# VectorE's operations for the second chunk's heads, issued behind those on the features of the first two slots

## The chip, the cores and the metric

The kernel runs on one core of a Trainium2 chip. What counts is the time of one execution on the device, in microseconds (us). Three runs of the kernel before took 885.66, 886.93 and 889.05 us; the median is 886.93.

A core has five engines, each with its own in-order queue: TensorE (PE in the profile: matrix products, with PEld for its weight loads), VectorE (DVE), ScalarE (ACT), GpSimd (POOL) and SyncE (SP), which here issues the loads and stores. An instruction starts when it has reached the head of its engine's queue and the semaphores that it waits for have been raised; all behind it on that engine wait with it.

## The reference

Two steps follow each other. The first is attention over 8 batches, 8 heads, 576 positions of 64 features; heads 0 to 3 look at the last 32 positions (local), heads 4 to 7 at the positions with the same remainder by 32 (strided). The second is a feed-forward layer on the 4608 tokens.

```python
scores = scale * np.matmul(q, k.transpose(0, 1, 3, 2))
mask_local = (rel >= 0) & (rel < stride)
mask_strided = (rel >= 0) & (pos[None, :] % stride == pos[:, None] % stride)
scores = np.where(masks[None, :, :, :], scores, -1000000000.0)
scores = scores - np.max(scores, axis=-1, keepdims=True)
attn = np.exp(scores)
attn = attn / (np.sum(attn, axis=-1, keepdims=True) + 1e-09)
x = np.matmul(attn, v)            # then laid out as 4608 tokens x 512
h = np.maximum(x @ w_in, 0.0)     # 512 -> 2048
out = h * h @ w_out               # 2048 -> 512
```

The weights w_in and w_out arrive as 64-bit floats.

## The kernel before

**Tiling.** The 4608 tokens are cut into 12 chunks of 384, each made of two segments of 192 positions of one batch. For each chunk the heads give four tiles: xlh, xll (local heads, high and low part) and xsh, xsl (strided heads). A number in 32 bits is split into a high part that TensorE's fast 32-bit format holds and a low part, the rest; a product is done as three: high with high, high weight with low x, low weight with high x. So `up` issues 12 products for one slot of 128 features (four 128-row pieces of x times three), and `down` issues 9 for one slot (three token tiles times three).

**Slots.** A chunk has 16 slots j of 128 features. `up(c, j)` makes h_j (on TensorE, L458), its squared Relu, the high part gh (ScalarE, L471) and the low part gl (VectorE, L472). `down` adds slot j's part to y (L485), two slots later in chunk 0. In chunk 0 the squared Relu is split: ScalarE makes the Relu (L466), VectorE multiplies it with h (L467), then ScalarE casts gh from that. In later chunks ScalarE does both (L469, L470).

**Weights.** They are converted on the chip during chunk 0, from 64-bit halves to high and low parts, by `convert`: ScalarE scales (L154) and prepares the low word (L166), VectorE joins the two (L169), ScalarE casts the high part (L172), GpSimd subtracts for the low part (L173). Six steps of it run ahead of the slots, then WRATE = 2 steps per slot, each issued on ScalarE behind the slot's gh. Weight pieces come in the order w_0 (of w_in), w_1, w_0 (of w_out) and so on; a piece is converted in two halves of 512 columns.

**Heads of chunk 0** are made ahead of everything, by `pe_pair` on TensorE. `heads_end` holds the last instructions of that part by engine: a for ScalarE, g for GpSimd, s for SyncE, v for VectorE.

**Heads of chunk 1.** Its local heads again go through `pe_pair` (`local`). Its strided heads go through `strided`, which uses VectorE and GpSimd and runs once per segment: for each of the six positions i of a segment in its lane GpSimd multiplies q with the keys up to i (L408), VectorE sums over the features (L409); then maximum, difference, exponential, sum and normalisation (L414 to L421); then GpSimd multiplies values with weights (L430) and VectorE sums (L431). The result is transposed (L437), cast into xsh (L441) and xsl (L442). The products of L408 and of L430 share two buffers (`prod`, bufs=2): the third product can only be written when the first has been summed. A segment's data come by one load (L388).

**What sets the order.** The program is traced in Python order, and a scheduler then orders each engine's queue; it works with estimates of times, and moves instructions between the traced places where data allow. `issue_after(ins)` binds: what is traced within it stands behind `ins` on that engine's queue. `behind(ins, gen)` applies it, for every engine in a dictionary, to each step of a generator. Up to slot LATER = 3 chunk 1's heads are not yet traced; from there on a share of them is traced in each slot, but bound only behind `heads_end`, so the scheduler may put them earlier, into the places of slots 0 to 2.

**In the names of the order** h_0 to h_15 are chunk 0's features, gh_0 and gl_0 their two parts, raw_... a weight piece on its way and w_... the converted one, z_... the prepared low word, sc_2, pq_2, pp_2 the scores, key products and value products of the first segment of chunk 1, sc_3, pq_3, pp_3 those of the second, and sc_4, pq_4 those of chunk 2. The last number of a name only tells tiles apart.

Of the kernel before, what the change touches and what calls it, by code (L numbers as in the profile page):

```python
# [49 lines left out]
def f32(ap):  # L50
    return ap.bitcast(F32)
# [23 lines left out]
def ranges(c):  # L75

    res = []
    for s, (b, g) in enumerate(SEGS[c]):
        if res and res[-1][0] == b and res[-1][2] == SI * g:
            res[-1][2] += SI  # L80
        else:
            res.append([b, SI * g, SI * (g + 1), SEG * s])
    return res
# [3 lines left out]
def attn_moe(ctx: ExitStack, tc, qk_l, v_l, qk_d, v_d, qk_p, v_p, f_s, q_s, k_s, v_s, w_in, w_out, masks, eye, out):  # L87
    nc = tc.nc
# [13 lines left out]
    def psum(i, nm):  # L102

        return ps.tile([P, 512], F32, name=nm, tag=f"ps{i}")
# [17 lines left out]
    last = {}  # L122
# [325 lines left out]
    def up(c, j):  # L448
        x = xt[c]
        p, o = divmod(j, 2)  # L450
        ph = psum((c * NFT + j) % 3, f"h{c}_{j}")
        n = 0
        for kt in range(4):
            kind, kk = "ls"[kt // 2], kt % 2
            xh, xl = x[kind, "h"][:, kk, :], x[kind, "l"][:, kk, :]
            wsl = slice(kt * 256 + o * P, kt * 256 + (o + 1) * P)
            for w, xx in ((wi[p][0], xh), (wi[p][0], xl), (wi[p][1], xh)):
                done = nc.tensor.matmul(ph[:, :TC], w[:, wsl], xx, start=n == 0, stop=n == 11)  # L458
                n += 1
        gh = gpool.tile([P, TC], F32R, name=f"gh{c}_{j}", tag="gh")  # L460
        gl = gpool.tile([P, TC], F32R, name=f"gl{c}_{j}", tag="gl")
        g = ph[:, :TC]
        if c == 0:

            r = p_t[j % 2].rearrange("p w q -> p (w q)")
            nc.scalar.activation(r, g, AF.Relu)  # L466
            nc.vector.scalar_tensor_tensor(out=g, in0=g, scalar=0.0, in1=r, op0=ALU.max, op1=ALU.mult)  # L467
        else:
            nc.scalar.activation(g, g, AF.Relu)  # L469
            nc.scalar.activation(g, g, AF.Square)  # L470
        last["gh"] = nc.scalar.copy(gh, g)  # L471
        nc.vector.tensor_sub(gl, g, f32(gh))  # L472
        g_tiles[c, j] = gh, gl
        return done

    def down(c, j):
        gh, gl = g_tiles.pop((c, j))
        p, o = divmod(j, 2)
        if j == 0:
            y_ps[c] = [ps_y.tile([P, DM], F32, name=f"y{c}_{t}", tag="psy") for t in range(NTT)]  # L480
        wsl = slice(o * DM, (o + 1) * DM)
        for t in range(NTT):
            sl = slice(t * P, (t + 1) * P)
            for k, (g, w) in enumerate(((gh, wo[p][0]), (gh, wo[p][1]), (gl, wo[p][0]))):
                done = nc.tensor.matmul(y_ps[c][t], g[:, sl], w[:, wsl], start=j == 0 and k == 0, stop=j == NFT - 1 and k == 2)  # L485
        if j == NFT - 1:
            for t in range(NTT):
                y = ypool.tile([P, DM], F32, name=f"ysb{c}_{t}", tag="ysb")
                (nc.scalar.copy if t == 1 else nc.vector.tensor_copy)(y, y_ps[c][t])
                nc.sync.dma_start(out=out[c * TC + t * P : c * TC + (t + 1) * P, :], in_=y)  # L490
        return done


    def run(gen):
        for _ in gen:
            pass

    def behind(ins, gen):

        while True:  # L500
            with ExitStack() as st:
                for i in ins.values():
                    st.enter_context(tc.issue_after(i.ins))
                try:
                    k = next(gen)
                except StopIteration:
                    return
            yield k
# [25 lines left out]
    def local(c):  # L534
        heads = [pair_at(c, pr, True, pr, "3") for pr in range(2)]
        for h in (0, 0, 1, 0, 1, 0, 0, 1, 1, 1):
            next(heads[h])
            yield
# [15 lines left out]
    def take(c, which):  # L554

        if NPLAIN <= c < NCHUNK:
            for h in map(int, which):
                if (c, h) not in heads:
                    heads[c, h] = pe_head(c, h)
                with ExitStack() as st:  # L560
                    for i in (last["pe"], *(weights_end.values() if c == NPLAIN else ())):
                        st.enter_context(tc.issue_after(i.ins))
                    last.pop("mm", None)
                    next(heads[c, h])
                    last["pe"] = last.get("mm", last["pe"])
# [51 lines left out]
    heads_end = {e: last[e] for e in "agsv"}  # L617
# [3 lines left out]
    for s in range(NS + 2):  # L621
        c, j = divmod(s, NFT)
        if s < NFT:
            up(c, j)
            if s >= 2:
                last["pe"] = down(*divmod(s - 2, NFT))

        elif s % 2 == 0:
            before, between, rest = plan[j // 2]
            for part, slots, two in (up, (s, s + 1), before), (down, (s - 2, s - 1), between):  # L630
                take(c + 1, two)
                with tc.issue_after(last["pe"].ins):
                    for i in slots:
                        if 0 <= i < NS:
                            last["mm"] = part(*divmod(i, NFT))
                last["pe"] = last["mm"]
            take(c + 1, rest)
        if j == NFT - 2:
            take(c + 2, "010")
        if c == 0:  # L640

            weights = behind({"a": last["gh"]}, ungated)
            for _ in range(WRATE):
                if next(weights, "end") != "end":
                    weights_end = {e: last[e] for e in "agsv"}
        if s == LATER:
            zbank = (4,)
        if s == NFT - 1:
            for t in p_t:
                nc.gpsimd.memset(t, 0.0)  # L650
        if c + 1 < NCHUNK and s >= LATER:
            j0 = LATER if c == 0 else 0
            if j == j0:
                lo, st = local(c + 1) if c == 0 else iter(()), strided(c + 1)
                if c == 0:
                    lo, st = behind(heads_end, lo), behind(heads_end, st)
                if c == 1:
                    st = behind(weights_end, st)
                cost = sum(2 * sum(range(i0 + 1, i1 + 1)) + 10 for _, i0, i1, _ in ranges(c + 1))
                dl = ds = 0  # L660
            fl, fs = ((j + 1 - j0) / n for n in SPREAD[min(c, 1)])
            while dl < fl * 10 and next(lo, "end") != "end":
                dl += 1
            while ds < fs * cost:
                k = next(st, "end")
                if k == "end":
                    break
                ds += k
            if j == NFT - 1:
                run(lo)  # L670
                run(st)
# [76 lines left out]
```

## Time and profile before

| | |
|---|---|
| median of three runs | 886.93 us |
| the profiled execution | 886.95 us |
| its span, first to last instruction | 885.2 us |
| mean granted TensorE clock | 0.993 |
| PE busy | 871.1 us (98%) |
| VectorE, ScalarE, GpSimd busy | 640.3, 572.1, 677.3 us |

The profile is that of one execution. The share of busy time is an average over all stages; the first 47 us (loads, heads of chunk 0, first slots) differ from the rest. In the row of the granted clock 1.00 is full speed (2.4 GHz) and 0.50 half of it. Times of instructions count from the start of the span. A row of the timeline may merge neighbours of one kind (x6); its second number then is the time from the first start to the last end.

### The profile page before, as it was taken

To read this page: it belongs to the slowest core of one execution; us is meant where nothing else is said; L and a number is where in the kernel's file an instruction comes from. 1 tells how busy PE (TensorE), PEld (TensorE's weight loads), DVE (VectorE), ACT (ScalarE), POOL (GpSimd) and SP (SyncE) were. 2 spreads that over 40 slices of the span, in tenths; PEclk is the share of its full clock that TensorE was granted. 3 is DMA by queue.
4 is the path that set the end of the run, shared out by engine and by line. 5 is a ranking of instruction groups with operands and counts; after the bars stand their busy time and mean duration, and the time that the engine had idled before them with its cause. 6 is when DMAs were issued, how large, how long until landed. Compare 5 with 4: busy or idle time off the path is not lost.

```text
span 885.2 us, 14792 instructions
## 1 busy us (share of the span) xinstructions
PE 871.1 (98%) x4744; PEld 792.5 (90%) x4744; DVE 640.3 (72%) x1820; ACT 572.1 (65%) x1510; POOL 677.3 (77%) x722
## 2 busy tenths in 40 slices
PE   8799999999999999999999999999999999999997
PEld 7688899999999999989899999999999999998996
DVE  5579677877877878878779778778787887883111
ACT  5799876666666666757757747656666665664332
POOL 4689887878987989889888988997998899782000
PEclk9899999999999999999999999999999999999999
DMA  9943441323023123104102302312021121000000
GB/s 347 361 149 107 154 150 40 103 83 113 26 71 103 45 80 107 43 13 147 47 13 79 99 29 74 90 44 74 29 98 61 31 70 61 7 2 8 29 1 36
DMA packets 26797, 71.40 MB, mean 81 GB/s; under 512 B 2976, under 2 KB 8736, under 8 KB 25184
## 3 DMA queue, kind: packets, MB, share of 16 engines
q1 hardware_dynamic: 26432, 70.14, 24.0%
q8 instruction: 37, 0.61, 0.3%
q10 hardware_dynamic: 288, 0.33, 0.1%
q14 instruction: 40, 0.33, 0.1%
HBM read 61.01 MB, written 9.44 MB: 80 GB/s over the span
## 4 chain that ended last, share of the span: by engine, by line
PE 96%; DMA 2%; ACT 1%; POOL 1%; DVE 0%; issue 0%; DVEq 0%; POOLq 0%; ACTq 0%
PE h L458 45%; PE y L485 45%; PE s L234 2%; PE o L280 2%; DMA qk<-qk_d 2%; ACT e L341 1%; PE w_ps L580 1%; PE b L317 1%; PE b L363 0%; POOL pq L408 0%; POOL w L173 0%; PE b L355 0%; DVE e L322 0%; ACT raw L154 0%; DVEq L739 0%
## 5 line engine op out<-in xcount | busy, mean ns | idle before, releaser
L485 PE MATMUL y<-w,gh 128*128 128x512 f32 x1152 | 357.5, 392 | 2.0 <-ACT gh L471 2.0
L485 PEld LDWEIGHTS y<-w,gh 128*128 128x128 f32 x1152 | 212.5, 188 | 42.2 <-ACT gh L471 2.3
L458 PE MATMUL h<-xlh,w 128*128 128x384 f32 x768 | 230.8, 341 | 1.8 <-DVE raw L169 1.8
L458 PE MATMUL h<-xsh,w 128*128 128x384 f32 x768 | 226.1, 335 | 0.0
L485 PE MATMUL y<-w,gl 128*128 128x512 f32 x576 | 224.7, 393 | 0.0
L430 POOL TENSOR_TENSOR pp<-vs,sc 128x448 f32<-128x448 f32 (+10 forms) x192 | 189.9, 1014 | 38.1 <-DVE qs L431 19.2
L408 POOL TENSOR_TENSOR pq<-ks,qs 128x512 f32<-128x512 f32 (+2 forms) x192 | 197.9, 1050 | 17.6 <-DVE sc L409 13.8
L472 DVE TENSOR_TENSOR gl<-h,gh 128x384 fp32r<-128x384 f32 x192 | 105.5, 550 | 81.3 <-ACT gh L471 80.1
L409 DVE TENSOR_REDUCE sc<-pq 128x8 f32<-128x512 f32 (+4 forms) x228 | 119.8, 535 | 50.0 <-POOL pq L408 46.9
L471 ACT CAST gh<-h 128x384 fp32r<-128x384 f32 x192 | 91.6, 478 | 98.5 <-PE y L485 96.0
L469 ACT ACTIVATE h<-h 128x384 f32<-128x384 f32 x176 | 82.9, 471 | 109.7 <-PE h L458 109.2
L458 PEld LDWEIGHTS h<-xlh,w 128*128 128x128 f32 x768 | 143.2, 190 | 4.9 <-DVE raw L169 2.0
L458 PEld LDWEIGHTS h<-xsh,w 128*128 128x128 f32 x768 | 141.9, 188 | 0.2
L431 DVE TENSOR_REDUCE qs<-pp 128x64 f32<-128x448 f32 (+11 forms) x192 | 106.7, 563 | 32.4 <-POOL pp L430 30.6
L458 PE MATMUL h<-xll,w 128*128 128x384 f32 x384 | 130.0, 339 | 0.0
L485 PEld LDWEIGHTS y<-w,gl 128*128 128x128 f32 x576 | 108.5, 188 | 23.0
L458 PE MATMUL h<-xsl,w 128*128 128x384 f32 x384 | 128.4, 335 | 0.0
L470 ACT ACTIVATE h<-h 128x384 f32<-128x384 f32 x176 | 83.3, 473 | 3.6
L259 DVE STREAM_TRANSPOSE p_t<-e 32x128 f32<-32x128 f32 x240 | 72.2, 301 | 10.5 <-ACT e L248 6.2
L458 PEld LDWEIGHTS h<-xll,w 128*128 128x128 f32 x384 | 73.1, 190 | 2.2
L458 PEld LDWEIGHTS h<-xsl,w 128*128 128x128 f32 x384 | 72.2, 188 | 0.1
L243 ACT ACTIVATE e<-e,nm 96x128 f32<-96x128 f32 x160 | 62.6, 393 | 12.9 <-DVE nm L226 11.1
(87 smaller groups left out, 1080.4 us busy)
## 6 DMA issues: line engine op xcount, KB each, us to landing
qk<-qk_l SPq DMA_DIRECT2D x24, 400.0 KB, 3.2
y<-ysb SPq DMA_DIRECT2D x36, 256.0 KB, 3.4
raw<-w_in SPq DMA_DIRECT2D x7, 1024.0 KB, 11.4
qk<-qk_l SPq DMA_DIRECT2D x16, 416.0 KB, 3.2
vs<-v_s SPq DMA_DIRECT2D x10, 576.0 KB, 4.1
raw<-w_out SPq DMA_DIRECT2D x5, 1024.0 KB, 13.3
v<-v_l SPq DMA_DIRECT2D x40, 128.0 KB, 2.1
ks<-k_s SPq DMA_DIRECT2D x8, 576.0 KB, 3.8
```

Source lines behind the costliest of these rows:

```text
L243: nc.scalar.activation(e[:QC, cut(w)], e[:QC, cut(w)], AF.Exp, bias=nmax[:QC, w : w + 1], scale=-1.0, accum_out=ssum[:QC, w, :1])
L259: nc.vector.transpose(out=pt[STR * k : STR * (k + 1), :, STR * r : STR * (r + 1)], in_=e.rearrange("p (w k) -> p w k", k=KW)[STR * r : STR ...
L408: nc.gpsimd.tensor_mul(pv, kt[:, a : a + m, :], qt[:, i - i0 : i - i0 + 1, :].broadcast_to([P, m, D]))
L409: nc.vector.tensor_reduce(out=sc[:, i - i0, a : a + m], in_=pv, op=ALU.add, axis=AX.X)
L430: nc.gpsimd.tensor_mul(pv, vt[:, a : a + nd, :n], sc[:, il : il + 1, :n].broadcast_to([P, nd, n]))
L431: nc.vector.tensor_reduce(out=ot[:, il, a : a + nd], in_=pv, op=ALU.add, axis=AX.X)
L458: done = nc.tensor.matmul(ph[:, :TC], w[:, wsl], xx, start=n == 0, stop=n == 11)
L469: nc.scalar.activation(g, g, AF.Relu)
L470: nc.scalar.activation(g, g, AF.Square)
L471: last["gh"] = nc.scalar.copy(gh, g)
L472: nc.vector.tensor_sub(gl, g, f32(gh))
L485: done = nc.tensor.matmul(y_ps[c][t], g[:, sl], w[:, wsl], start=j == 0 and k == 0, stop=j == NFT - 1 and k == 2)
```

## The change

At the end of slot 1 a second dictionary is made from `heads_end`: for VectorE it holds the instruction that makes gl of slot 1 instead of the last one of chunk 0's heads. Chunk 1's heads, local and strided, are bound behind it. For the other three engines nothing differs in the dictionary.

```diff
@@ up
         last["gh"] = nc.scalar.copy(gh, g)
-        nc.vector.tensor_sub(gl, g, f32(gh))
+        last["gl"] = nc.vector.tensor_sub(gl, g, f32(gh))
@@ the loop over slots
+        if s == 1:
+
+            slot_end = heads_end | {"v": last["gl"]}
         if s == LATER:
             zbank = (4,)
@@
                 if c == 0:
-                    lo, st = behind(heads_end, lo), behind(heads_end, st)
+                    lo, st = behind(slot_end, lo), behind(slot_end, st)
```

The scheduler orders all queues anew from this. VectorE's queue at the first slots of chunk 0, of before (-) and now (+):

```order
 L169 SCALAR_TENSOR_TENSOR raw_196<-raw_196,z_512_512 128x512
-L409 TENSOR_REDUCE sc_2_680<-pq_2_0_0_682 128x1
-L409 TENSOR_REDUCE sc_2_680<-pq_2_1_0_685 128x2
-L409 TENSOR_REDUCE sc_2_680<-pq_2_2_0_688 128x3
-L409 TENSOR_REDUCE sc_2_680<-pq_2_3_0_691 128x4
-L409 TENSOR_REDUCE sc_2_680<-pq_2_4_0_694 128x5
 L467 SCALAR_TENSOR_TENSOR h_0_517<-h_0_517,p_t_90 128x384
-L409 TENSOR_REDUCE sc_2_680<-pq_2_5_0_755 128x6
 L467 SCALAR_TENSOR_TENSOR h_1_548<-h_1_548,p_t_91 128x384
-L414 TENSOR_REDUCE mx_2_758<-sc_2_680 128x6
 L472 TENSOR_TENSOR gl_0_531<-h_0_517,gh_0_530 128x384
 L169 SCALAR_TENSOR_TENSOR raw_261<-raw_261,z_0_537 128x512
```

The first segment's six score reductions and its maximum leave this place; they now stand behind gl_1, spread among the weights' L169 and the features of slots 2 and 3.

GpSimd's queue at the same place:

```order
 L408 TENSOR_TENSOR pq_2_0_0_682<-qkvs_2_678 128x64
 L408 TENSOR_TENSOR pq_2_1_0_685<-qkvs_2_678 128x128
+L173 TENSOR_TENSOR w_0_505<-raw_196,w_0_505 128x512
+L173 TENSOR_TENSOR w_2_536<-raw_261,w_2_536 128x512
 L408 TENSOR_TENSOR pq_2_2_0_688<-qkvs_2_678 128x192
 L408 TENSOR_TENSOR pq_2_3_0_691<-qkvs_2_678 128x256
+L173 TENSOR_TENSOR w_2_536<-raw_261,w_2_536 128x512
 L408 TENSOR_TENSOR pq_2_4_0_694<-qkvs_2_678 128x320
 L408 TENSOR_TENSOR pq_2_5_0_755<-qkvs_2_678 128x384
-L173 TENSOR_TENSOR w_0_505<-raw_196,w_0_505 128x512
-L173 TENSOR_TENSOR w_2_536<-raw_261,w_2_536 128x512 x2
+L173 TENSOR_TENSOR w_1_567<-raw_263,w_1_567 128x512 x2
```

Three weight conversions have moved in among the key products. Behind this piece the conversions of w_1, w_3 and half of w_2 now follow each other, and the value products pp_2 stand behind them.

GpSimd's queue at the end of chunk 0, where the second segment's xsl is made:

```order
+L653 MEMSET p_t_90 128x384
+L653 MEMSET p_t_91 128x384
 L173 TENSOR_TENSOR w_7_1249<-raw_0_1075,w_7_1249 128x512
 L400 MEMSET sc_4_1472 128x108
 L218 TENSOR_TENSOR kx_0_1340<-qk_0_1329,kx_0_1340 128x448
+L220 TENSOR_TENSOR qx_0_1339<-qk_0_1329,qx_0_1339 64x384
 L408 TENSOR_TENSOR pq_4_0_0_1474<-qkvs_4_1470 128x64
 L408 TENSOR_TENSOR pq_4_1_0_1477<-qkvs_4_1470 128x128
-L220 TENSOR_TENSOR qx_0_1339<-qk_0_1329,qx_0_1339 64x384
 L255 TENSOR_TENSOR vx_0_1580<-v_0_1330,vx_0_1580 128x4x64
+L173 TENSOR_TENSOR w_7_1249<-raw_512_1077,w_7_1249 128x512
 L442 TENSOR_TENSOR xsl_886<-qkvs_3_951,xsh_885 128x2x192
```

The two memsets and the last weight conversion, which stood behind this L442, now stand in front of it. Elsewhere the order differs too: on PE's queue three y products of slot 2 now stand inside h_4, in front of its last four products, and on SyncE's the second segment's load (L388) stands behind the load of raw_803 instead of in front of it. The new file has three lines more, so L650 of before is L653 there.

## Rows read from the trace of the kernel before

**Rows 1.** Page: busy us (share of the span) and number of instructions by engine.

```profile
PE 871.1 (98%) x4744; PEld 792.5 (90%) x4744; DVE 640.3 (72%) x1820; ACT 572.1 (65%) x1510; POOL 677.3 (77%) x722
```

**Rows 2.** All waits of PE from 28 us on: total, times, longest, us.

```profile
PE y L485 <- ACT gh L471: 2.0, 1, 2.0
PE h L458 <- DVE raw L169: 1.8, 1, 1.8
```

**Rows 3.** Timeline of PE: start, duration, instruction, idle before it and its releaser.

```profile
18.44 1.25 PE L363 MATMUL b<-pt,v 128*64 128x96 f32 x16 [0.70 <-ACT pt L356]
...
42.51 1.94 PE L485 MATMUL y<-w,gh 128*128 128x512 f32 x6 [1.98 <-ACT gh L471]
...
48.37 1.55 PE L485 MATMUL y<-w,gh 128*128 128x512 f32 x6
...
50.45 0.33 PE L458 MATMUL h<-xlh,w 128*128 128x384 f32 x1
```

**Rows 4.** Stretches: PE, PEld, DVE, ACT, POOL busy; granted clock, DMA share, GB/s.

```profile
0.00:20.00 20.00, 16.79 (x212) 15.34 (x213) 10.30 (x23) 11.18 (x41) 6.91 (x17) 1.00 0.93 338
...
40.50:42.50 2.00, 0.03 (x1) 0.00 (x0) 1.59 (x5) 0.53 (x2) 1.40 (x2) 1.00 0.59 223
42.50:45.50 3.00, 2.99 (x9) 2.36 (x10) 2.83 (x6) 3.00 (x6) 1.33 (x1) 0.70 0.04 15
45.50:47.10 1.60, 1.60 (x6) 1.58 (x5) 1.35 (x4) 1.60 (x5) 0.53 (x1) 0.50 0.00 0
```

**Rows 5.** Timeline of VectorE in front of the first slot's feature.

```profile
40.98 0.49 DVE L409 TENSOR_REDUCE sc<-pq 128x5 f32<-128x320 f32 x1 [0.41 <-POOL pq L408]
41.38 0.56 DVE L467 SCALAR_TENSOR_TENSOR h<-h,p_t 128x384 f32<-128x384 f32 x1
```

**Rows 6.** Timeline of ScalarE: Relu, cast of gh_0, four of the weight casts.

```profile
39.52 0.87 ACT L466 ACTIVATE p_t<-h 128x384 f32<-128x384 f32 x2 [3.00 <-PE h L458]
41.98 0.48 ACT L471 CAST gh<-h 128x384 fp32r<-128x384 f32 x1 [1.58 <-DVE h L467]
...
42.91 0.65 ACT L172 CAST w<-raw 128x512 fp32r<-128x512 f32 x1
...
45.81 0.68 ACT L172 CAST w<-raw 128x512 fp32r<-128x512 f32 x1
...
49.98 0.65 ACT L172 CAST w<-raw 128x512 fp32r<-128x512 f32 x1
...
56.52 0.71 ACT L172 CAST w<-raw 128x512 fp32r<-128x512 f32 x1
```

**Rows 7.** Timeline of GpSimd: the first key products, and around the second L442.

```profile
38.12 3.78 POOL L408 TENSOR_TENSOR pq<-qkvs 128x64 f32<-128x64 f32 x6
43.64 1.33 POOL L173 TENSOR_TENSOR w<-raw,w 128x512 fp32r<-128x512 f32 x1 [1.74 <-ACT w L172]
...
109.87 1.02 POOL L442 TENSOR_TENSOR xsl<-qkvs,xsh 128x384 fp32r<-128x384 f32 x1
...
111.76 1.31 POOL L173 TENSOR_TENSOR w<-raw,w 128x512 fp32r<-128x512 f32 x1
113.01 0.42 POOL L650 MEMSET p_t<- 128x384 f32 x1
```

**Rows 8.** Stretches, as in rows 4; POOL is the fifth busy time.

```profile
38.00:110.90 72.90, 70.92 (x388) 62.44 (x387) 56.70 (x118) 62.99 (x118) 62.64 (x70) 0.98 0.43 146
59.50:110.90 51.40, 51.40 (x299) 45.28 (x298) 38.75 (x79) 44.59 (x85) 45.62 (x48) 1.00 0.47 158
```

**Rows 9.** Timeline of PE: chunk 1's first product with the second segment's xsl.

```profile
111.44 0.33 PE L458 MATMUL h<-xsl,w 128*128 128x384 f32 x1
```

**Rows 10.** Timeline of VectorE: L421 in the first segment, and in chunk 2.

```profile
48.91 1.29 DVE L421 TENSOR_TENSOR sc<-sc,sm 128x36 f32<-128x36 f32 x1
...
120.09 0.20 DVE L421 TENSOR_TENSOR sc<-sc,sm 128x36 f32<-128x36 f32 x1
```

**Rows 11.** Timeline of SyncE: the second segment's load.

```profile
62.91 0.33 SPq L388 DMA_DIRECT2D qkvs<-f_s  x1
```

## Prediction

> **What bounds the kernel now.** I read the busy shares first: TensorE (PE) is busy for 98% of the span [rows 1], so only time in which PE waits or runs at a lower clock can be won. The table of waits, asked for PE from 28 us on, then has two rows, and one bears on this change: 2.0 us in front of the first y product, ended by ScalarE's cast of gh (L471) [rows 2]. The timeline of PE shows the place: the first y product starts at 42.51 after 1.98 us of idleness [rows 3]. The stretches tell what follows: granted clock 1.00 while PE idles, 0.70 over 42.5 to 45.5, 0.50 over 45.5 to 47.1, which is half of the full 2.4 GHz [rows 4]. In lost time that is 3.0 x 0.30 + 1.6 x 0.50 = 1.7 us. So the place holds 2.0 + 1.7 = 3.7 us, and no version of this edit can win more. Nine y products took 2.08 us at full clock (48.37 to 50.45) [rows 3], which is the scale of it.
>
> **What stands in the way there.** ScalarE finished the Relu of h_0 at about 40.0 (two in 0.87 us from 39.52) [rows 6]. VectorE's product for h_0 (L467) started only at 41.38, behind reductions (L409) of the second chunk's first segment, the last of which itself waited 0.41 us for GpSimd [rows 5]. The cast followed at 41.98 [rows 6].
>
> **The change, part by part.**
>
> First, VectorE. Six L409, one L414 and one L415 leave the place in front of and among the features of slots 0 and 1. L467 on h_0 can start at 40.05 instead of 41.38: 1.33 us earlier, and so can the cast (40.65) and the first y product (41.18). PE's wait shrinks from 1.98 to about 0.65 us. ScalarE is an unbroken queue behind that cast, so the weight casts move forward by the same 1.33 us, no more.
>
> Second, the clock. A wait of 0.70 us at 18.44 [rows 3] lies in a stretch at 1.00 [rows 4], so I take it that 0.65 us leaves the clock up and the 1.7 us are won too; if not, 0.
>
> Third, a new wait. PE now gets to h_4 three microseconds early, but the weights only 1.3 us early. The first y products of slot 2, which now stand inside h_4, need the cast that started at 49.98 and took 0.65 [rows 6]: it ends near 49.2, PE is there at 48.8. Cost 0.5 us. Lead of PE from there on: 1.3 + 1.7 - 0.5 = 2.5 us.
>
> Fourth, GpSimd, which pays. Its products (L408) have two buffers, so from the third one on each needs a reduction that VectorE now runs only behind gl_1 (about 45.4). Before, all six ran in one piece from 38.12 [rows 7]. Now GpSimd stands idle after two of them, from 38.9 until the cast for w_0_505 ends (42.91 + 0.65 - 1.33 = 42.2) [rows 6]: 3.4 us. Again from 43.6 until the cast for w_2_536 ends (45.81 + 0.68 - 1.33 = 45.2): 1.6 us. Then it has five conversions (L173) of 1.3 us and four products (3.0 us of the 3.78) in hand, until 54.6, and waits for the cast of 56.52 (over at 55.9): 1.3 us. That makes 6.3 us of idleness. All weights come in time, since the order lets the conversions pass; what slips is the segment's value products (L430), by some 10 us, and with them everything of the second segment.
>
> What hides this in chunk 0 is that nothing on PE needs the strided heads until chunk 1. There the cover ends: PE's first product with the second segment's low part (xsl, L458) started at 111.44 [rows 9], and the L442 that makes it ran from 109.87 to 110.89 [rows 7]. The slack is 0.55 us. When does this L442 end now? From 38.0 to 110.9 GpSimd was busy for 62.64 us [rows 8]. In front of L442 the new order also puts the conversion that ran at 111.76 (1.31 us) and the two memsets (0.42 each) [rows 7]: 64.8 us. With the 6.3 us of idleness it ends at 38.0 + 64.8 + 6.3 = 109.1 if GpSimd never waits again after 56. If it waits as much as it did from 59.5 to 110.9 (51.40 - 45.62 = 5.8 us [rows 8]) it ends at 114.9. I take 3.2 us, nearer the middle: those waits were mostly for casts, which a GpSimd that is behind with its heads finds done; left are the first segment's softmax, on which its value products wait, the later load of the second segment, and the reductions that now stand on VectorE behind a weight half that has yet to land (near 96 us). So L442 ends at 112.3.
>
> PE arrives there at 111.44 - 2.5 = 108.9 and waits 3.4 us for it. Behind the waiting product stand all of chunk 1's features, since PE runs them in order, and behind these every later y. PE resumes at 112.35, 0.9 us later than before: whatever it won at 41 us is given back here. After that wait, longer than the 1.98 us that were followed by the lower clock, I expect one more stretch at half clock, at the price measured above, 1.7 us (bounds: 0, and 2.6 if the wait falls so that the lower level holds half as long again).
>
> **Sum.** The profiled execution took 886.95 us (span 885.2 and 1.75 around it), as good as the median of 886.93. Change: +0.9 (PE resumes later in chunk 1) + 1.7 (clock) = +2.6: 889.5 us. From 112 us on PE had no wait before [rows 2], GpSimd is soon ahead of its former times again since it has that conversion behind it, and I take nothing further.
>
> **A rule weighed.** The normalising product L421 (36 elements a lane) took 1.29 us at 48.91 and 0.20 us at 120.09 [rows 10]. Beside the first GpSimd was at work, in the 2.27 us before the second one it idled. The Trainium skill, SBUF — State Buffer, section Who interferes with whom, has it that a VectorE instruction with two SBUF inputs and a GpSimd instruction that reads SBUF exclude each other for a whole instruction. By that rule the trace agrees, and L421 of the first segment would end as GpSimd's conversion ends: the 0.5 us that my 3.2 holds for it would go, and the sum would be 889.0. By the row's 1.29 it is 889.5, which I keep.
>
> **Rivals.** (a) GpSimd catches up. For it: it idled for 10.3 of 72.9 us before [rows 8], more than the new idleness of 6.3. Against it: it must also do 2.15 us more in front of L442, and its slack there was 0.55. If it waits nowhere after 56 us, L442 ends at 109.1, PE hardly waits, and the lead stays but for 0.2 us: 884.6.
>
> (b) GpSimd keeps all its old waits, at one place above all: the second segment's data. Its load was issued at 62.91 [rows 11]; it waits for the first segment's L442, which slips by 10 us or more, and on SyncE's queue it now stands behind another weight load. Each microsecond by which it lands after GpSimd wants it is idle time on the only queue that feeds L442. With L442 at 114.9, PE resumes 3.5 us late and pays the 1.7: 892.1; it counts as slower from L442 at 114.1 on.
>
> (c) The edit does not do what it says: the first y product still waits about 2 us, for something that I took to be ready. PE then has no lead, the casts come 1.3 us later than in the forecast, L442 ends near 113.6: +2.2 + 1.7 = 890.8.
>
> (d) The clock does not fall after the new wait: 887.8.
>
> **How the numbers follow.** 0.5% is 4.4 us, about what a measurement of this kernel can tell from no change: slower is above 891.4, faster below 882.5. Chances: forecast with its spread of the later waits and of the clock (886.5 to 891) 0.62; (a) 0.10; (b) 0.17; (c) 0.04; (d) 0.07. Faster needs more than the 3.7 us that the place holds: 0.02. Slower is (b) and a tail of (c) and the forecast: 0.19. The rest is 0.79. The range of 8 in 10 goes from 885.6, between (a) and (d), to 892.1, the whole of (b)'s price.
>
> **What would show it.** Right: L467 on h_0 near 40.05, the y wait near 0.65, clock 1.00 through 42.5 to 47.1; GpSimd idle 3.4 us before the conversion at about 42.3; a short wait of PE near 49 for L172; the table of PE's waits led by h<-xsl waiting for L442, 2.5 to 4.5 us long, ending near 112.3, and half clock close behind it. Wrong: no wait for L442 (then (a), and the later idleness of GpSimd was covered), a wait for xsh or its cast instead, or PE waiting in later chunks, which would mean that GpSimd's delay lives on.

## The result and the profile after

Twenty runs of the changed kernel have a median of 889.32 us (886.90 to 890.47), twenty of the kernel before, beside them, 887.02 (885.60 to 889.21). The ratio is 1.0020, with a 95% interval of 1.0011 to 1.0028: slower by 0.2%, which is under the 0.5% of the prediction's "same". Forecast was 889.5. The profiled execution took 890.13 us (span 888.3), among the longer ones of the change.

All waits of PE from 28 us on, in the changed kernel (total, times, longest):

```profile
PE h L458 <- POOL xsl L442: 3.3, 1, 3.3
PE h L458 <- DVE raw L169: 1.3, 1, 1.3
PE y L485 <- ACT gh L471: 0.7, 1, 0.7
```

Against [rows 2], the y wait shrank from 2.0 to 0.7, and a wait of 3.3 us for L442 heads the table. The timeline of PE at the two places:

```profile
41.08 1.64 PE L485 MATMUL y<-w,gh 128*128 128x512 f32 x6 [0.65 <-ACT gh L471]
...
112.25 0.69 PE L458 MATMUL h<-xsl,w 128*128 128x384 f32 x1 [3.34 <-POOL xsl L442]
```

PE was at the first product with xsl at 112.25 - 3.34 = 108.91, which is 2.53 us ahead of [rows 9] (111.44), and left it 0.81 us behind. The stretches (PE, PEld, DVE, ACT, POOL busy; granted clock, DMA share, GB/s), for [rows 4] and for the second place:

```profile
42.50:45.50 3.00, 3.00 (x17) 2.85 (x17) 1.77 (x5) 3.00 (x7) 1.44 (x2) 1.00 0.01 3
45.50:47.10 1.60, 1.60 (x8) 1.30 (x8) 0.86 (x3) 1.60 (x4) 1.60 (x3) 1.00 0.02 5
...
112.25:117.60 5.35, 5.35 (x17) 5.12 (x18) 3.33 (x13) 2.28 (x5) 3.17 (x5) 0.50 0.66 218
```

The 0.70 and 0.50 of the kernel before have become 1.00; 5.35 us at 0.50 have come behind the new wait, which is 2.7 us of lost time.

GpSimd at the end of chunk 0 (start, duration, instruction, idle before it), and ScalarE's cast of xsh, from which the subtraction could start:

```profile
106.25 1.17 POOL L218 TENSOR_TENSOR kx<-qk,kx 128x448 fp32r<-128x448 f32 x1
107.49 1.01 POOL L220 TENSOR_TENSOR qx<-qk,qx 64x384 fp32r<-64x384 f32 x1
108.58 0.73 POOL L408 TENSOR_TENSOR pq<-qkvs 128x64 f32<-128x64 f32 x2
109.27 0.72 POOL L255 TENSOR_TENSOR vx<-v,vx 128x256 fp32r<-128x256 f32 x1
109.95 1.29 POOL L173 TENSOR_TENSOR w<-raw,w 128x512 fp32r<-128x512 f32 x1
111.20 0.99 POOL L442 TENSOR_TENSOR xsl<-qkvs,xsh 128x384 fp32r<-128x384 f32 x1
```

```profile
106.50 0.52 ACT L441 CAST xsh<-qkvs 128x384 fp32r<-128x384 f32 x1
```

The reader is to see that L442's input was there at 107.02, that GpSimd was hardly idle between 106.25 and 111.20, and that nothing of what it did there is needed by the product that PE waits for: kx, qx, pq and vx belong to chunk 2's heads, the conversion to w_7.

### The profile page after: what moved, and what is told of

Read it like the earlier page. It is cut to its first block, busy times and chain, and to the rows that moved or that the text cites. A ratio compares the mean times of both kernels' runs of the same rounds, so it can differ in the third digit from the quotient of the medians.

```text
span 888.3 us, 14790 instructions
## 1 busy us (share of the span) xinstructions
PE 874.8 (98%) x4744; PEld 795.3 (90%) x4744; DVE 640.1 (72%) x1820; ACT 570.2 (64%) x1510; POOL 676.2 (76%) x722
## 4 chain that ended last, share of the span: by engine, by line
PE 93%; ACT 4%; DVE 1%; POOL 1%; issue 0%; DVEq 0%; POOLq 0%; ACTq 0%
PE h L458 44%; PE y L485 43%; PE s L234 2%; PE o L280 2%; ACT raw L154 1%; ACT e L341 1%; PE b L317 1%; PE w_ps L580 1%; ACT z L166 1%; ACT w L172 1%; DVE sc L415 0%; PE b L374 0%; ACT pt L356 0%; PE b L355 0%; PE b L363 0%
## 5 line engine op out<-in xcount | busy, mean ns | idle before, releaser
L458 PE MATMUL h<-xlh,w 128*128 128x384 f32 x768 | 229.8, 340 | 1.3 <-DVE raw L169 1.3
L458 PE MATMUL h<-xsh,w 128*128 128x384 f32 x768 | 226.3, 336 | 0.0
L408 POOL TENSOR_TENSOR pq<-ks,qs 128x512 f32<-128x512 f32 (+2 forms) x192 | 197.8, 1049 | 21.3 <-DVE sc L409 17.0
L458 PEld LDWEIGHTS h<-xlh,w 128*128 128x128 f32 x768 | 142.0, 189 | 4.0 <-DVE raw L169 1.5
L458 PEld LDWEIGHTS h<-xsh,w 128*128 128x128 f32 x768 | 142.2, 189 | 0.5
L458 PE MATMUL h<-xsl,w 128*128 128x384 f32 x384 | 129.3, 337 | 3.3 <-POOL xsl L442 3.3
L458 PE MATMUL h<-xll,w 128*128 128x384 f32 x384 | 129.4, 337 | 0.0
L458 PEld LDWEIGHTS h<-xsl,w 128*128 128x128 f32 x384 | 72.6, 189 | 3.9 <-POOL xsl L442 3.7
L458 PEld LDWEIGHTS h<-xll,w 128*128 128x128 f32 x384 | 72.5, 189 | 2.2
```

Source lines behind the costliest of these rows:

```text
L408: nc.gpsimd.tensor_mul(pv, kt[:, a : a + m, :], qt[:, i - i0 : i - i0 + 1, :].broadcast_to([P, m, D]))
```

## The experiments

Theories and rivals have letters. A: the lead of 2.5 us is lost because of what stands in front of L442 on GpSimd (order). B: it is lost because GpSimd idles behind reductions that now come later (idleness, on which my fourth step laid the weight). D: the lead is lost anyway at the next wait. E, F and G are told where they come up. The kernel before, run beside them, had medians of 886.95 (first four experiments) and 886.98 us (next four); the last two are single executions.

**1. xsl of the second segment on VectorE.**

```diff
-            nc.gpsimd.tensor_sub(x["s", "l"][:, :, cols], src, ...)
+            (nc.vector if c == 1 and col else nc.gpsimd).tensor_sub(x["s", "l"][:, :, cols], src, ...)
```

> The changed kernel, with the second segment's xsl (L442) made by VectorE instead of GpSimd. Theory A (order): PE is 2.5 us ahead after the first slots and loses it only because this subtraction, whose input xsh was cast by 107.0, stood on GpSimd behind 4.2 us of other work. Then PE waits for nothing at xsl (it is there at 108.9), the clock stays at 1.00 over 108.5 to 118, and the time is 890.1 - 3.3 (wait) - 2.7 (half clock) = 884.1 us; chunk 2's heads may take up to 1 us of that. Theory D (the lead is lost anyway): the wait moves to xsh or to chunk 2's heads, over 2 us long, and the time stays at 887 or more.

Measured: 884.41 us, ratio to the kernel before 0.9977 (0.9968 to 0.9986). VectorE's and PE's rows at the place:

```profile
107.26 0.76 DVE L442 TENSOR_TENSOR xsl<-qkvs,xsh 128x384 fp32r<-128x384 f32 x1 [0.34 <-ACT xsh L441]
```

```profile
108.59 0.51 PE L458 MATMUL h<-xsh,w 128*128 128x384 f32 x2
108.94 0.33 PE L458 MATMUL h<-xsl,w 128*128 128x384 f32 x1
109.11 0.51 PE L458 MATMUL h<-xsh,w 128*128 128x384 f32 x2
```

PE passes without a wait, the clock is 1.00 in every stretch from 106 to 122 us, and no other wait takes the place: D falls. GpSimd's order up to 112 us is that of the change but for the one subtraction. Moving one instruction of 1 us turns a change that costs 2.3 us into one that wins 2.5.

**2. Only the order: L442 stays on GpSimd, other work is bound behind it.**

```diff
+            last["xsl"] = nc.gpsimd.tensor_sub(x["s", "l"][:, :, cols], src, ...)
...
-            take(c + 2, "010")
+            with tc.issue_after(last["xsl"].ins):
+                take(c + 2, "010")
...
-            for t in p_t:
-                nc.gpsimd.memset(t, 0.0)
+            with tc.issue_after(last["xsl"].ins):
+                for t in p_t:
+                    nc.gpsimd.memset(t, 0.0)
...
-            weights = behind({"a": last["gh"]}, ungated)
+            weights = behind({"a": last["gh"]} | ({"g": last["xsl"]} if s > 14 else {}), ungated)
...
-                    st = behind(weights_end, st)
+                    st = behind(weights_end | {"g": last["xsl"]}, st)
```

> The changed kernel, L442 still on GpSimd, but the two memsets, chunk 2's heads and its key products bound behind it. Theory A (order): L442 ends near 109.6, behind the xsh cast and one weight conversion; PE waits about 0.6 us for it and up to 0.5 us for chunk 2's heads, no half clock: 885 us. Theory B (idleness): what makes L442 late is GpSimd standing idle behind reductions that VectorE now runs later (its products have two buffers); that idleness is untouched, so a wait of 2.5 us or more stays in front of xsl and the time is 888 to 889.5 us.

Measured: 885.40 us, ratio 0.9991 (0.9982 to 1.0000). GpSimd:

```profile
105.58 0.74 POOL L255 TENSOR_TENSOR vx<-v,vx 128x256 fp32r<-128x256 f32 x1
106.81 1.31 POOL L173 TENSOR_TENSOR w<-raw,w 128x512 fp32r<-128x512 f32 x1 [0.48 <-ACT w L172]
108.08 1.01 POOL L442 TENSOR_TENSOR xsl<-qkvs,xsh 128x384 fp32r<-128x384 f32 x1
```

L442 ends at 109.09; PE's first xsl product starts at 109.15, about 0.3 us late, and 0.2 us are lost to chunk 2's heads. No half clock. The order alone takes the wait away, with GpSimd's early idleness untouched (3.45 us before its first conversion, at 42.34): A holds, B's price does not. The edit does more than undo what the change did to this order: the conversion stays in front of L442, and kx, qx and the two key products, which stood in front of it in the kernel before too, now stand behind it.

**3. Only the idleness: the first segment's products in room of their own.** The products from the third on go into chunk 1's x tiles, which are not in use yet; they are rounded there.

```diff
+                    if c == 1 and b == SEGS[1][0][0] and i >= 2:
+                        spare = x_tiles(c)["s", "l" if i < 5 else "h"].rearrange("p a t -> p (a t)")
+                        prod = spare[:, (0, 192, 448, 0)[i - 2] :]
+                    else:
+                        prod = spool.tile([P, JH * D], F32, ..., tag="prod", bufs=2)
```

> The changed kernel, but the products of the first segment from the third on (L408) are written into room of their own (chunk 1's x tiles, not yet in use; the products are rounded there), so that GpSimd need not wait for reductions between 40 and 46. Theory B (idleness): GpSimd is done 4 to 5 us earlier, no wait for xsl, no half clock: 884 us. Theory A (order): the idleness comes back as waits for the weight casts of the next slots, L442 keeps its place behind the same other work and ends about 1.2 us earlier; PE still waits 2 to 3 us for it and the half clock stays: 888 us.

Measured: 888.27 us, ratio 1.0004 (0.9993 to 1.0015). GpSimd at the first slots, then at the end of the chunk (L412 is this file's L408, L446 its L442):

```profile
38.13 0.74 POOL L412 TENSOR_TENSOR pq<-qkvs 128x64 f32<-128x64 f32 x2
38.83 2.12 POOL L412 TENSOR_TENSOR xsl<-qkvs 128x192 fp32r<-128x192 f32 x3
40.90 1.03 POOL L412 TENSOR_TENSOR xsh<-qkvs 128x384 fp32r<-128x384 f32 x1
42.23 1.33 POOL L173 TENSOR_TENSOR w<-raw,w 128x512 fp32r<-128x512 f32 x1 [0.31 <-ACT w L172]
45.12 1.33 POOL L173 TENSOR_TENSOR w<-raw,w 128x512 fp32r<-128x512 f32 x1 [1.56 <-ACT w L172]
47.25 1.33 POOL L173 TENSOR_TENSOR w<-raw,w 128x512 fp32r<-128x512 f32 x1 [0.80 <-ACT w L172]
...
109.84 0.99 POOL L446 TENSOR_TENSOR xsl<-qkvs,xsh 128x384 fp32r<-128x384 f32 x1
```

All six products run in one piece again, and the idleness comes back as waits for casts (0.31, 1.56, 0.80 and on). The subtraction ends at 110.83 instead of 112.19, 1.36 us earlier, PE still waits 2.2 us for it and the half clock follows. B is refuted as the main cause: the idle time at 40 to 46 is worth 1.4 us at the far end, not the 4 to 5 us that B had for it (in the change it is 2.14 + 1.56 = 3.7 us long).

**4. PE kept busy through the wait.** Twenty products with zeros, which add nothing, in front of h_0's products with xsh.

```diff
+NFILL = 20
...
+            if c == 1 and j == 0 and kt == 2:
+                zero = p_t[1].rearrange("p w q -> p (w q)").bitcast(BF16)
+                for _ in range(NFILL):
+                    nc.tensor.matmul(ph[:, :TC], zero[:, :P], zero[:, :TC], start=False, stop=False)
```

> The changed kernel, with 20 products with zeros (they add nothing) issued in h_0 of chunk 1 in front of the products with xsh, so that PE is busy through the wait for xsl. The wait's end is unchanged (near 112.3). If the clock fell because PE idled there, it stays at 1.00 over 109 to 118 and the time falls by what the half clock cost in the profile, 5.4 us at half, 2.7 us: 887.4 for a run like the profiled one of the change, 887 in the median. If the lower clock has another cause, 889.3 as before the edit.

Measured: 888.08 us, ratio to the kernel before 1.0018 (1.0009 to 1.0027); the profiled run 888.01. PE (L463 is this file's L458):

```profile
107.34 3.42 PE L461 MATMUL h<-p_t 128*128 128x384 bf16 x20
...
112.17 0.44 PE L463 MATMUL h<-xsl,w 128*128 128x384 f32 x1
```

```profile
112.00:114.00 2.00, 1.99 (x11) 1.84 (x11) 0.77 (x2) 0.63 (x2) 2.00 (x4) 1.00 0.91 263
114.00:116.00 2.00, 2.00 (x12) 1.72 (x11) 1.76 (x8) 1.98 (x5) 1.81 (x3) 1.00 0.79 295
```

The first xsl product starts where it did (112.17 against 112.25), the clock is 1.00 throughout, and the time falls by 2.1 us against the profiled run of the change and by 1.2 us in the medians. The lower clock came from the idleness, and it is a cost of its own beside the wait. Expected were 887.4 for the profiled run and 887 in the median, so 0.6 and 1.1 us less were won than a half clock of 2.7 us would give; where the rest is, is not shown. What is left against the kernel before, 888.08 - 886.95 = 1.1 us, is for the most part the 0.7 us by which PE still resumes later (112.17 against 111.44).

**5. xsl on VectorE, without the change** (the edit of the first experiment, made to the kernel before). Rival E: VectorE is the better place in any case.

> The kernel before (heads bound behind heads_end), with the second segment's xsl made by VectorE. Theory A (the subtraction is on the path only because the change makes it later): before the change PE reached it 0.55 us after it was done, so nothing is won: 886.5 to 887.5 us, y wait 2.0 us and half clock at 42.5 to 47.1 as before. Rival E (VectorE is simply the better place, the change has no part in the gain of the first run): 884.4 us here too.

Measured: 888.02 us, ratio 1.0013 (1.0000 to 1.0026). Nothing is won, so E falls. The profile surprised in another place, the first y product:

```profile
43.65 2.93 PE L485 MATMUL y<-w,gh 128*128 128x512 f32 x6 [3.26 <-ACT gh L471]
```

A wait of 3.26 us, where [rows 3] have 1.98. Runs 9 and 10 look into this.

**6. Bound behind gl of slot 0.** One character. Rival F: any binding behind the features costs GpSimd so much that xsl is late.

```diff
-        if s == 1:
+        if s == 0:
             slot_end = heads_end | {"v": last["gl"]}
```

> The changed kernel, but chunk 1's heads bound behind gl of slot 0 instead of slot 1; GpSimd keeps xsl. Theory A: the first y product is won as in the change (wait 0.65 us, clock 1.00), GpSimd gets its product buffers back 3 us earlier and only one conversion of the weights moves in among the key products; at the end of chunk 0 the last weight conversion stays behind L442, which ends near 109.2, where PE arrives at 109.3: no wait for xsl, 884.5 to 885.5 us. Rival F (any binding behind the features costs GpSimd so much that xsl is late): a wait of 2 us or more and half clock, 888 or more.

Measured: 885.08 us, ratio 0.9977 (0.9968 to 0.9985). GpSimd, then PE:

```profile
107.94 0.42 POOL L653 MEMSET p_t<- 128x384 f32 x1
108.31 1.01 POOL L442 TENSOR_TENSOR xsl<-qkvs,xsh 128x384 fp32r<-128x384 f32 x1
```

```profile
109.38 0.44 PE L458 MATMUL h<-xsl,w 128*128 128x384 f32 x1 [0.24 <-POOL xsl L442]
```

The y wait is 0.7 us as in the change, and this order leaves the last weight conversion behind L442. F falls. But the order is not all of it. GpSimd from 38.0 to the start of L442:

```profile
38.00:108.31 70.31, 69.56 (x387) 60.60 (x386) 55.81 (x118) 62.27 (x118) 63.59 (x70) 1.00 0.43 145
```

In the change it was busy for 64.65 us of 73.20 in front of L442, here for 63.59 of 70.31: 1.06 us less work and 1.83 us less idleness. So idleness has a price too: here it is the larger part of the 2.89 us by which L442 starts earlier (108.31 against 111.20).

**7. Bound behind gl of slot 2** (`if s == 2`).

> The changed kernel, bound behind gl of slot 2, later than in the change. Theory A: GpSimd is held back longer, L442 ends near 114.4 and PE waits 3.7 us for it, after 0.6 to 1.0 us more at the weight conversions of slots 10 to 13, then half clock: 891.5 us. Theory D (what counts is the lead at the first slots alone): as the change or better, 887 to 889.5.

Measured: 889.90 us, ratio 1.0034 (1.0022 to 1.0046).

```profile
112.51 0.44 PE L458 MATMUL h<-xsl,w 128*128 128x384 f32 x1 [3.49 <-POOL xsl L442]
```

```profile
112.50:117.00 4.50, 4.49 (x17) 4.31 (x18) 2.74 (x10) 1.97 (x5) 2.99 (x4) 0.62 0.77 261
```

The wait and the half clock came (0.38 x 4.5 = 1.7 us), the 0.6 to 1.0 us at the conversions of slots 10 to 13 did not, and L442 ended 1.9 us before the expected 114.4, so 891.5 was too high by 1.6. L442 ended at 112.46, almost as in the change (112.19), although the first segment's L442 ended 6.0 us later (78.59 against 72.57): a first segment that slips takes the second one along by little.

**8. The edits of experiments 1 and 3 together.**

> The changed kernel with xsl of the second segment on VectorE and the spare room for the first segment's products (those are rounded there). If both act as in their own runs, PE's short wait near 49 goes too, since in this order the y products of slot 2 don't stand inside h_4: 0.3 to 0.6 us under the first run, 884.0 us. If that wait is made up for elsewhere: 884.4.

Measured: 884.00 us, ratio 0.9971 (0.9960 to 0.9982). The intervals of this and of experiment 1 overlap; that the short wait near 49 us is worth anything is not shown.

**9 and 10. The change and the kernel before, profiled again.** Rival G: the waits vary with how the heads of chunk 0 go.

> The changed kernel itself, a second profile. Runs of it lie between 886.9 and 890.5 us. If the wait for xsl is a matter of the order (theory A), it is 3.2 to 3.5 us again, and whatever the time differs by from the first profile's 890.13 is the length of the half clock behind it (0 to 2.7 us). If the wait itself varies with how the first loads land (rival G), it differs by over 1 us.

> The kernel before itself, a second profile. Its runs lie between 885.6 and 890.4 us. In the run with xsl on VectorE and without the change, PE waited 3.3 us for the first y product instead of 2.0, GpSimd's key products having begun at 39.3 instead of 38.1. If that is how the kernel before varies (rival G), this profile shows either pair: 2.0 us and about 886.9, or 3.3 us and about 889; if not, the wait is 2.0 whatever the time.

Measured: the change 890.54 us, the kernel before 886.94 us. PE's waits in the change, then in the kernel before:

```profile
42.35 0.98 PE L485 MATMUL y<-w,gh 128*128 128x512 f32 x3 [0.65 <-ACT gh L471]
...
113.53 0.69 PE L458 MATMUL h<-xsl,w 128*128 128x384 f32 x1 [3.33 <-POOL xsl L442]
```

```profile
43.63 1.65 PE L485 MATMUL y<-w,gh 128*128 128x512 f32 x6 [3.25 <-ACT gh L471]
```

The wait for xsl is 3.33 us again, A as expected. From the first y product on, the change lies 1.27 us later here (42.35 against 41.08); the heads are not later (key products from 39.27, against 39.31), but over 35 to 38 us, in the first features, PE's clock was 0.50 here and 1.00 there. The half clock behind the wait is shorter here:

```profile
113.53:117.20 3.67, 3.67 (x13) 3.63 (x14) 1.89 (x5) 1.05 (x3) 2.98 (x4) 0.54 0.87 283
```

That is 3.67 x 0.46 = 1.7 us, so the nearly equal times of the two profiles of the change are made of different parts. For the kernel before G holds in part, and my pairing of wait and time was wrong. The wait is 2.0 or 3.25 us, and the longer one came in the two profiles (this one and experiment 5, which is the kernel before but for xsl) where PE had the clock of 0.50 from 20 to 30 us, but with it the time was 889.4 once and 886.94 once. The difference lies for the most part in the clock behind the wait; the stretches of run 10, in which nothing is below 1.00:

```profile
42.50:45.50 3.00, 1.86 (x8) 1.56 (x9) 3.00 (x8) 2.40 (x4) 1.26 (x2) 1.00 0.01 3
45.50:47.10 1.60, 1.60 (x11) 1.52 (x10) 1.47 (x3) 1.60 (x5) 0.59 (x1) 1.00 0.00 0
```

In experiment 5 the same two stretches, behind an equal wait, had 0.58 and 0.50.

## Why the prediction was right, and where its reasons were not

| step | predicted | measured |
|---|---|---|
| 1: L467 on h_0 / first y product / wait | 40.05 / 41.18 / 0.65 | 39.94 / 41.08 / 0.65 |
| 2: clock over 42.5 to 47.1 | 1.00 | 1.00 |
| 3: wait near 49 | 0.5 | 0.1 |
| lead of PE at xsl | 2.5 | 2.53 |
| 4: L442 ends / PE waits / resumes later by | 112.3 / 3.4 / 0.9 | 112.19 / 3.34 / 0.81 |
| 5: half clock behind it | 1.7 (0 to 2.6) | 2.7, and 1.7 in the second profile |
| time | 889.5 | 889.32 (profiled: 890.13) |

The mechanism came as forecast: PE won its lead, met an L442 that was not ready, and paid a half clock behind the wait. The median lies 0.2 us from the forecast, but that is luck in part. The sum adds up parts of a profiled run, and there it is 0.6 us too low: PE resumed 0.81 us later and lost 2.7 us to the clock, where the sum had 0.9 and 1.7 and at most 2.6 for the clock, and the two profiled runs differ by 3.18. Runs of the changed kernel go from 886.90 to 890.47.

Steps 1 and 2 came as worked out. The y wait was 0.6 to 0.7 us in every profile that has the change's binding in any form, and the two stretches behind it had a clock of 1.00. The row of step 1 on VectorE:

```profile
39.94 1.03 DVE L467 SCALAR_TENSOR_TENSOR h<-h,p_t 128x384 f32<-128x384 f32 x2 [2.13 <-ACT p_t L466]
```

Step 3 was mis-sized. PE was busy for 0.89 of the 1.00 us from 48.3 to 49.3, so 0.1 us was lost and not 0.5: the cast, which by the prediction's own rows would have ended at 49.98 + 0.65 - 1.33 = 49.3, ended at 49.06. The lead of 2.5 us came all the same. It was 3.03 us at h_4 (47.42 against the 50.45 of [rows 3]) and 2.53 at xsl; 0.4 us went between the two in a way that no row here shows, so the lead is right by two errors.

```profile
48.30:49.30 1.00, 0.89 (x5) 0.57 (x5) 1.00 (x4) 1.00 (x3) 1.00 (x2) 1.00 0.00 0
```

Step 4 gave the right end of L442, but with two terms off that cancel: it had 64.8 us of work up to that end and 6.3 + 3.2 = 9.5 us of idleness; measured are 64.65 + 0.99 = 65.64 (more than forecast, since in this profile the conversions ahead of the key products ran until 39.2) and 8.55. And its words put the price on the 6.3 us of new idleness, which is not what makes L442 late. At the first two places that idleness was, in the change:

```profile
42.21 1.33 POOL L173 TENSOR_TENSOR w<-raw,w 128x512 fp32r<-128x512 f32 x1 [2.14 <-ACT w L172]
45.09 1.33 POOL L173 TENSOR_TENSOR w<-raw,w 128x512 fp32r<-128x512 f32 x1 [1.56 <-ACT w L172]
```

Forecast were 3.4 and 1.6. The first is 3.45 to 3.50 us in experiment 2 and in run 9, so its size was right; it is less in this profile, in which the key products began 1.2 us late and the cast that ends the idleness did not. But the kernel before idled as well. GpSimd from 38.0 to the start of L442, in the kernel before, in run 10 (the kernel before, its key products from 39.28) and in the change (key products from 39.31):

```profile
38.00:109.87 71.87, 69.89 (x382) 61.41 (x381) 56.32 (x118) 62.99 (x118) 61.61 (x68) 0.98 0.42 145
```

```profile
38.00:109.85 71.85, 68.46 (x381) 59.89 (x380) 56.16 (x118) 62.92 (x118) 62.67 (x69) 1.00 0.40 141
```

```profile
38.00:111.20 73.20, 70.14 (x390) 61.27 (x389) 57.84 (x118) 62.46 (x118) 64.65 (x71) 1.00 0.44 147
```

Idle were 71.87 - 61.61 = 10.26 and 71.85 - 62.67 = 9.18 us before, and 73.20 - 64.65 = 8.55 us in the change: less, not more. Run 10 is the better partner, with heads as late as in this profile of the change. Against it GpSimd was busy for 1.98 us more, and 1.98 - 0.63 = 1.35 is the whole delay of L442 (111.20 against 109.85). The conversion and the two memsets that the new order puts in front are 1.29 + 0.79 = 2.08 us, which is that work. In run 9, the second profile of the change, the work is the same (64.64 us up to 112.48) and the idleness 9.84, 0.66 more than in run 10. So what I had as a side item, "in front of L442 the new order also puts" 2.15 us, is what delays L442 in the first profile and three quarters of its delay in the second (1.97 of 112.48 - 109.85 = 2.63 us), and the new idleness near 40 us stands in the place of idleness that GpSimd had before too (1.74 us up to 43.64 [rows 7], and more behind it).

That delay is not the whole wait. If L442 had ended at 110.89 as in the kernel before, PE, there at 108.91, would still have waited 1.98 of its 3.34 us. What kept L442 at that time is work that stood in front of it before the change too, and cost nothing as long as PE came at 111.44: kx, qx, pq and vx above are 1.17 + 1.01 + 0.73 + 0.72 = 3.6 us. Experiment 2 took the memsets and most of this from in front of L442, and the wait went; experiment 3 worked on the early idleness, and 2.2 of 3.3 us stayed.

Step 5 had the right sign for a reason that does not hold. It said that a wait longer than 1.98 us is followed by the lower clock. Run 10 has 3.25 us of waiting and no half clock. Behind the xsl wait itself the clock fell in all four profiles that have one over 2 us (the change twice, experiments 3 and 7), with 1.7 to 2.7 us lost where it is worked out above, and experiment 4 shows that it is paid because PE idles. What decides whether it falls is open.

The rule that I weighed is not decided by the row that I named. L421 of the first segment took 0.19 us at 58.84, but GpSimd had idled since 58.21, so the two did not meet. Nor does the time decide: the sum of 889.0 that the rule led to is 0.3 us from the measured 889.32, mine 0.2. In the second segment they did meet. L421 took 1.24 us at 95.37 and ended at 96.61, with the conversion that GpSimd had begun at 95.24 (over at 96.55). And L415 (VectorE, then GpSimd):

```profile
90.34 3.53 DVE L415 TENSOR_TENSOR sc<-sc,mx 128x36 f32<-128x36 f32 x1
```

```profile
89.95 3.87 POOL L173 TENSOR_TENSOR w<-raw,w 128x512 fp32r<-128x512 f32 x3
```

An operation on 36 elements a lane takes 3.53 us and ends at 93.87, with the last of three conversions (93.82). The Trainium skill, SBUF — State Buffer, section Who interferes with whom, has the loser of the shared ports block for the whole instruction of the winner; L421 agrees with this, while L415 was held over three instructions in a row. In the kernel before, the same L415, at 82.85 beside three such conversions (3.86 us from 82.86), took 1.37 us. What decides between one and three is open, and what the 3.53 us cost the kernel no run shows.

Of the rivals, (a) did not happen, but experiments 1 and 6 show its time: 884.6 was its price, 884.4 and 885.1 were measured where PE waits for xsl not at all or for 0.24 us. The mechanism of (b) did not: the second segment's load was issued at 72.60 and landed 3.6 us later, and GpSimd came to it at 78.06 without a wait. (c) is refuted by the 0.65, and (d) for this place by the stretches.

## What to carry to other kernels

Work that is moved out of one engine's critical place reorders the queues of the others; look for the instruction whose result is ready early and whose consumer stalls late, and compare the time at which its last input was there (here 107.02) with the time at which it started (111.20). A lead won early is only worth something if the next thing in line is early too, and work that was free behind a late consumer is not free behind an early one: the same edit was worth -2.5 us with one subtraction on another engine, and +2.3 us without. On the engine that bounds the kernel, count the clock behind a wait as a second price, and take its size from several profiles, not from one.

## What was not expected of the hardware

The lower clock does not follow from the length of the wait alone: 1.98 us (kernel before), 2.2 us (experiment 3) and 3.3 us (the change) were followed by it, 3.25 us in run 10 was not. And the length of the y wait, without the change, goes with the clock at which the heads of chunk 0 ran: over 20 to 30 us it was 0.50 in both profiles with a y wait of 3.25 or 3.26 us (run 10, experiment 5), and 1.00 and 0.66 (from 25 us) in the one with 1.98, where GpSimd's key products began at 38.12 instead of 39.28 or 39.29. With the heads bound behind the features the y wait no longer depends on this (0.65 us with either).

Also VectorE's L419, which adds a constant to 6 elements a lane, took 1.29 us at 56.96 beside a conversion of GpSimd, and 0.17 us at 94.61, when GpSimd idled.
